# Two operands of the seven-product layer kept in PSUM, and five output pieces in another order

## The chip, the cores and the metric

The kernel runs on one core of a Trainium2 chip. The time is device microseconds (us) of one execution; the median of several runs counts. All arithmetic that readers will meet is float32, much of it as pairs of a rounded high part and a low part.

## What is computed

The reference chains a retention (linear attention) layer, a dense mixture of four experts and a gated feed-forward layer:

```
x = attention(q, k, v, lam)                      # 1536 x 512
for e in range(4):                               # p: the normalized gate of a token
    h = max(x @ w1[e], 0)                        # 512 -> 1024
    out += p[:, e:e+1] * (h @ w2[e])             # 1024 -> 512
h = out @ w_in                                   # 512 -> 2048
return (h * sigmoid(h)) @ w_out                  # 2048 -> 512
```

## The kernel before, in words

The 1536 tokens are three blocks of 512. One block goes through the experts as plain products (phase "a", `gemm1` and `gemm2`), the other two go through them together (phase "c"); for the last layer these are phases "b" and "d". Each product is three matmuls of float32r parts: high by high, low by high, high by low.

In phases c and d the first layer of a pair of weight blocks is a Strassen form: seven products instead of eight, 1, 5, 6, 7, 3, 2, 4 in that order, each of six matmuls of 128x512 (`product`, L749). They accumulate in four PSUM banks that the program names x, y, z and v. Phase c has 16 pairs. The first eight (`pair_step`, L823) do the second layer plainly: eight pieces a pair, one for each of two token blocks t and four column blocks d (`down`, L794); piece d uses bank po`d`, and VectorE adds the bank to the accumulator one unit later (L817). The second eight pairs of phase c and all eight of phase d (`pair7`, L1008) use seven products for the second layer too (`down7`, L961). Its seven operands are sums of the activated blocks v, z, x, y. Operand 6 is v minus a sum, operand 4 is y minus operand 6.

Each operand is split in two steps by `operand` (L935): ScalarE rounds the source into `hhi` or `ohi` (L939), and VectorE, for operand 5 GpSimd, subtracts that from the source into `hlo` or `olo` (L941). Before the change operands 6 and 4 stand in the SBUF tile s2 (`second`, L1043, and L1126), so that VectorE's subtraction for them reads SBUF twice. In the profile this tile is called s, as are the SBUF copies of z and y that `copied` makes (L1019).

The banks change roles from pair to pair: the next pair's y is this pair's v, and the next v is this y (L1014). A pair begins its y with ScalarE's copy of x into that bank (L1053); the sixth product adds onto it. Between the products `filler` (L744) pops one second-layer piece from the list `fill` and then `unit` (L736) issues what is due, as the adding of a bank. The order within an engine is the order of the code (manual schedule): every engine runs its instructions in that order, and an instruction that waits holds those behind it.

At the first pair of the second form (pair 8 of phase c) `fill` holds 12 pieces: four with t = 0 of pair 6, d = 0 to 3, and eight of pair 7, t = 1 before t = 0. Line 1326 puts the four t = 1 pieces of pair 7 behind the first one, because `second_form` may close a pool of tiles after the last of them; one piece is popped behind each product.

Of the kernel before, what the change touches and what calls it, by code (L numbers as in the profile page):

```python
# [7 lines left out]
F32 = mybir.dt.float32  # L8
# [7 lines left out]
P = 128  # L16
# [9 lines left out]
TW = 512  # L26
# [13 lines left out]
def kernel(  # L40
# [189 lines left out]
    def flush():  # L230
        while pending:
            pending.pop(0)()
# [296 lines left out]
    tmp = {}  # L529
# [199 lines left out]
    fill = []  # L729
# [3 lines left out]
    def after(n, fn):  # L733
        due.append((clock[0] + n, fn))
# [9 lines left out]
    def filler():  # L744
        if fill:
            fill.pop(0)()
        unit()
# [187 lines left out]
    def operand(i, r, src, eng=nc.vector):  # L935

        kind = "h" if free["h"] and (r in (1, 5, 6) or not free["o"]) else "o"
        hi, lo, done = take(kind)
        nc.scalar.activation(out=hi, in_=src, func=AF.Copy)  # L939
        op_t[i, r] = hi, lo, done  # L940
        return lambda: eng.tensor_tensor(  # L941
            out=lo, in0=src, in1=hi.bitcast(F32), op=ALU.subtract
        )

    def vadd(out, a, b, op=ALU.add, eng=nc.vector):
        eng.tensor_tensor(out=out, in0=a, in1=b, op=op)  # L946
# [61 lines left out]
    def pair7(i, prepare, plan_n=None):  # L1008

        ph = now["ph"]  # L1010
        key = (ph, now["first"] + i)
        order = roles[0]
        x, y, z, v = (psum.tile([P, TW], F32, tag=f"ps{order[r]}", name=r) for r in "xyzv")
        roles[0] = {"x": order["z"], "y": order["v"], "z": order["x"], "v": order["y"]}  # L1014
        s, low, sig = {}, {}, {}

        def copied(name, src):
            s[name] = tmp["s"].tile([P, TW], F32, tag=f"s{name}", name=f"s{name}")
            nc.scalar.activation(out=s[name], in_=src, func=AF.Copy)  # L1019

        def gated(name, c):
            if ph == "d":
                sig[name] = tmp["d"].tile([P, TW], F32, tag="sg", name="sg", bufs=3)
                nc.scalar.activation(out=sig[name], in_=c, func=AF.Sigmoid)

        def times(name, c):
            to = c
            if name == "z":
                if ph == "c":
                    sig["z"] = tmp["d"].tile([P, TW], F32, tag="sg", name="sg")  # L1030
                to = sig["z"]
            if ph == "d":
                vadd(to, c, sig[name], ALU.mult)
            else:
                nc.vector.scalar_tensor_tensor(
                    out=to, in0=c, scalar=0.0, in1=gate_t["c", key[1] // 4, int(name in "vz")],
                    op0=ALU.max, op1=ALU.mult,
                )

        def high(r, c, eng=nc.vector):  # L1040
            low[r] = operand(i, r, c, eng)

        def second(a, b):  # L1043
            s[2] = tmp["d"].tile([P, TW], F32, tag="s2", name="s2")
            minus(s[2], a, b)

        def minus(to, a, b):
            vadd(to, a, b, ALU.subtract)

        plan = [  # L1050
            (
                (1, x, True),
                [lambda: nc.scalar.activation(out=y, in_=x, func=AF.Copy)],  # L1053
                0,
                [],
            ),
            ((5, z, True), [lambda: copied(5, z)], 1, []),
            ((6, y, False), [lambda: copied(16, y)], 1, []),
            (
                (7, y, False),  # L1060
                [lambda: vadd(v, y, s[5]), lambda: gated("v", v)],
                1,
                [lambda: times("v", v), lambda: high(3, v)],
            ),
            (
                (3, z, False),
                [lambda: vadd(z, z, s[16]), lambda: gated("z", z), lambda: low[3]()],
                1,
                [
                    lambda: times("z", z),  # L1070
                    lambda: minus(z, v, sig["z"]),
                ],
            ),
            (
                (2, x, False),
                [
                    lambda: gated("x", x),
                    lambda: high(7, z),
                    lambda: times("x", x),
                    lambda: high(1, x),  # L1080
                    lambda: low[7](),
                ],
                1,
                [
                    lambda: low[1](),
                    lambda: minus(sig["z"], sig["z"], x),
                    lambda: second(v, sig["z"]),
                ],
            ),
            (  # L1090
                (4, y, False),
                [
                    lambda: gated("y", y),
                    lambda: high(5, sig["z"], nc.gpsimd),
                    lambda: high(6, s[2]),
                    lambda: low[5](),
                ],
                2,
                [
                    lambda: times("y", y),  # L1100
                    lambda: high(2, y),
                    lambda: low[6](),
                    lambda: low[2](),
                ],
            ),
        ]
        for gap, ((r, to, begin), then, n, later) in enumerate(plan):
            if gap == 6 and i % 2:
                fill.extend(
                    (lambda m=m, d=d: down7(i // 2, m, d)) for m in range(7) for d in range(2)  # L1110
                )
            if plan_n:
                n = plan_n[gap]
            product(key, r, to, begin)
            for fn in then:
                fn()
            for job in prepare.get(gap, ()):
                job()
            for k in range(max(n, 1)):
                if n:  # L1120
                    filler()
                if k == 0:
                    for fn in later:
                        fn()

        minus(s[2], y, s[2])  # L1126
        after(2, lambda: high(4, s[2]))
        after(3, lambda: low[4]())

    def jobs_for(key, following):  # L1130

        jobs = {}
        if key[1] < SW:
            jobs[5 if key[1] < SW - 1 else 3] = [lambda: split_down(key)]
        if key[1]:
            jobs[0] = [lambda: left_second(key)]
        if following:
            jobs[2] = [lambda: left_sums(following)]
            jobs[4] = [lambda: left_first(following)]
        return jobs  # L1140
# [12 lines left out]
    with tc.manual_schedule():  # L1153
# [75 lines left out]
        for i in range(NN, na):  # L1229
            gi, f = steps["a"][i]  # L1230
# [72 lines left out]
        for i in range(NW):  # L1303
            jc = jobs_for(("c", i), ("c", i + 1) if i + 1 < NW else None)
            if i % 4 == 3:
                for gap, t in ((5, 1), (6, 0)):
                    jc.setdefault(gap, []).append(lambda t=t: load_gate("c", i // 4 + 1, t))
            if i < SW:
                for gap, fn in ((0, flush), (1, 0), (3, flush), (4, 0)):
                    if not fn:  # L1310
                        if (i, gap) == (0, 1) or i == SW - 1:
                            continue
                        fn = lambda: decode_next(True)
                    jc.setdefault(gap, []).append(fn)
                if i == SW - 2:
                    jc.setdefault(6, []).extend([flush, lambda: decode_next(True)])
                elif i == SW - 1:
                    jc[4].append(store_decoded)
                pair_step("c", i, jc)
                continue  # L1320
            if i == SW:
                flush()
                store_decoded()
                words.close()
                tmp["op"] = pool(ops, "opsp")
                fill[:] = fill[:1] + fill[4:8] + fill[1:4] + fill[8:]
                last_old = fill[4]
                fill[4] = lambda: (last_old(), second_form())
                jc[5] = jc.get(5, []) + [lambda: down_sums(0)]
                jc[6] = jc.get(6, []) + [lambda: down_sums(1)]  # L1330
            elif i == SW + 1:
                for gap, qs in ((0, [0]), (1, [1]), (3, [2]), (4, [3]), (6, [4, 5])):
                    jc.setdefault(gap, []).extend(lambda q=q: down_left(q) for q in qs)
            if i == NW - 1:
                jc[4] = [lambda: split_up(("b", 0), False)]
            pair7(i - SW, jc, {SW: [1] * 7, SW + 1: [0, 1, 1, 1, 1, 1, 2]}.get(i))

        for _ in range(3):
# [151 lines left out]
```

## Time and profile before

| what | us |
|---|---|
| median of 3 runs | 795.23 |
| the three runs | 788.44, 795.26, 795.23 |
| the profiled execution | 795.96 |
| its span, first to last instruction | 794.1 |
| TensorE busy in the span | 780.4 (98%) |
| VectorE busy | 571.3 (72%) |
| ScalarE busy | 363.4 (46%) |
| GpSimd busy | 504.8 (64%) |

The profiled execution has 1.86 us outside its span, and it is 0.73 us longer than the median. TensorE is named PE in the rows, VectorE DVE, ScalarE ACT, GpSimd POOL. Times in the rows are us from the span's start. A start and a length in a row of the timeline belong to one instruction or to several alike that follow each other; what stands in brackets is the idle time of the engine before it and what ended that.

### The profile page before, as it was taken

The page shows a single profiled execution, that of the slowest core. Times are in us where ns is not written, and L with a number is a line of the kernel's source. Part 1 is how long each engine was busy: PE and PEld are TensorE (multiplying, and loading weights), DVE is VectorE, ACT ScalarE, POOL GpSimd, SP SyncE. Part 2 cuts the span into 40 slices and gives each one's busy share as a digit, 9 for nine tenths or more (in the row PEclk, how much of TensorE's full clock was granted, in tenths as well). Part 3 has the DMA queues.
Part 4 walks back from the last instruction along what each step waited for, and adds up shares of the span by engine and source line. Part 5 has one row for each costly group of instructions (what it writes and reads, how often), then busy time and mean ns, then how long its engine had stood idle before and what let it go on. Part 6 is the DMA issues. An engine that isn't in the chain of part 4 may idle for free.

```text
span 794.1 us, 11059 instructions
## 1 busy us (share of the span) xinstructions
PE 780.4 (98%) x4038; PEld 646.4 (81%) x4038; DVE 571.3 (72%) x812; ACT 363.4 (46%) x648; POOL 504.8 (64%) x458
## 2 busy tenths in 40 slices
PE   8999999999999999998997999999999999999998
PEld 8888888888888888887886888888888787888886
DVE  7345587786586788888687887875455478888885
ACT  3323434334455344434352545454454476565651
POOL 3856655353775455555695898977777855666643
PEclk9999999999999999999999999999999999999999
DMA  8868668543244344333002120203867525232302
GB/s 296 317 226 249 223 214 294 197 170 101 93 146 133 132 151 142 132 104 108 29 27 79 40 95 26 80 27 136 294 237 286 181 92 173 66 128 81 123 1 107
DMA packets 39912, 113.89 MB, mean 143 GB/s; under 512 B 4482, under 2 KB 6706, under 8 KB 39858
## 3 DMA queue, kind: packets, MB, share of 16 engines
q1 hardware_dynamic: 39856, 113.18, 41.7%
q8 instruction: 32, 0.52, 0.3%
q14 instruction: 22, 0.18, 0.1%
q10 hardware_dynamic: 2, 0.00, 0.0%
HBM read 89.02 MB, written 24.14 MB: 143 GB/s over the span
## 4 chain that ended last, share of the span: by engine, by line
PE 80%; DVE 14%; ACT 3%; POOL 2%; issue 1%; ACTq 0%; POOLq 0%
PE po L981 19%; PE ph L553 17%; PE po L609 17%; PE y L755 9%; PE z L755 5%; PE x L755 5%; DVE acc L817 3%; PE po L803 3%; ACT hhi L782 2%; PE s L419 2%; PE xps L458 2%; DVE hlo L785 2%; DVE dec L213 1%; DVE dec L217 1%; DVE hlo L941 1%
## 5 line engine op out<-in xcount | busy, mean ns | idle before, releaser
L150 POOL TENSOR_TENSOR ub<-u,ua 128x1024 fp32r<-128x1024 f32 (+2 forms) x41 | 70.2, 1712 | 111.6 <-ACT ua L149 106.2
L150 POOL TENSOR_TENSOR dl<-d,dh 128x1024 fp32r<-128x1024 f32 (+1 forms) x33 | 78.5, 2381 | 24.6 <-ACT dh L149 24.5
L150 POOL TENSOR_TENSOR ub<-us,ua 128x1024 fp32r<-128x1024 f32 x23 | 56.0, 2435 | 28.7 <-ACT ua L149 28.7
L579 ACT ACTIVATE hhi<-ph 128x512 fp32r<-128x512 f32 x40 | 23.9, 599 | 104.1 <-DVE ph L573 85.1
L609 PE MATMUL po<-hhi,dh 128*128 128x512 f32 (+1 forms) x208 | 57.2, 379 | 0.0
L609 PE MATMUL po<-hhi,dl 128*128 128x512 f32 (+1 forms) x208 | 55.9, 373 | 0.0
L609 PE MATMUL po<-hlo,dh 128*128 128x512 f32 (+1 forms) x208 | 55.8, 372 | 0.0
L553 PE MATMUL ph<-xhi,ua 128*128 128x512 f32 (+1 forms) x208 | 53.3, 378 | 1.2 <-ACT ua L149 1.2
L803 PE MATMUL po<-hhi,dh 128*128 128x512 f32 x128 | 50.4, 394 | 2.6 <-DVE acc L817 2.6
L553 PE MATMUL ph<-xhi,ub 128*128 128x512 f32 (+1 forms) x208 | 52.3, 373 | 0.0
L553 PE MATMUL ph<-xlo,ua 128*128 128x512 f32 (+1 forms) x208 | 52.1, 372 | 0.0
L803 PE MATMUL po<-hhi,dl 128*128 128x512 f32 x128 | 50.3, 393 | 0.0
L803 PE MATMUL po<-hlo,dh 128*128 128x512 f32 x128 | 50.3, 393 | 0.0
L946 DVE TENSOR_TENSOR acc<-po,acc 128x512 f32<-128x512 f32 x56 | 37.9, 684 | 13.6 <-PE po L981 13.6
L580 DVE TENSOR_TENSOR hlo<-ph,hhi 128x512 fp32r<-128x512 f32 x40 | 27.7, 692 | 27.4 <-ACT hhi L579 27.4
L817 DVE TENSOR_TENSOR acc<-po,acc 128x512 f32<-128x512 f32 x56 | 37.0, 682 | 14.3 <-PE po L803 14.3
L553 PEld LDWEIGHTS ph<-xhi,ua 128*128 128x128 f32 x208 | 36.8, 188 | 8.9 <-ACT xhi L474 1.4
L946 DVE TENSOR_TENSOR a<-po,a 128x512 f32<-128x512 f32 (+1 forms) x50 | 33.6, 675 | 14.5 <-PE po L981 14.1
L149 ACT ACTIVATE dh<-d 128x1024 fp32r<-128x1024 f32 (+2 forms) x52 | 40.1, 792 | 7.6 <-PE po L609 3.1
L609 PEld LDWEIGHTS po<-hhi,dl 128*128 128x128 f32 x208 | 37.8, 188 | 7.0
L609 PEld LDWEIGHTS po<-hlo,dh 128*128 128x128 f32 x208 | 37.8, 188 | 7.0
L609 PEld LDWEIGHTS po<-hhi,dh 128*128 128x128 f32 x208 | 37.1, 188 | 7.5 <-issue 0.2
(218 smaller groups left out, 2182.0 us busy)
## 6 DMA issues: line engine op xcount, KB each, us to landing
u<-wts SPq DMA_DIRECT2D x32, 512.0 KB, 3.5
d<-wts SPq DMA_DIRECT2D x32, 512.0 KB, 4.2
words<-wts SPq DMA_DIRECT2D x32, 512.0 KB, 4.8
wd<-dec SPq DMA_DIRECT2D x32, 256.0 KB, 2.7
d<-wd SPq DMA_DIRECT2D x16, 512.0 KB, 3.6
qkt<-qk SPq DMA_DIRECT2D x12, 512.0 KB, 4.3
kvt<-kv SPq DMA_DIRECT2D x10, 512.0 KB, 4.8
u<-wd SPq DMA_DIRECT2D x8, 512.0 KB, 4.0
```

The source lines that it names most:

```text
L149: nc.scalar.activation(out=hi, in_=src, func=AF.Copy)
L150: eng.tensor_tensor(out=lo, in0=src, in1=hi.bitcast(F32), op=ALU.subtract)
L419: nc.tensor.matmul(s[t, p // n][:, p % n], lhsT=qkt[r, 1, p], rhs=qkt[r, 0, p], start=True, stop=True,)
L553: nc.tensor.matmul(pt[:, :n], lhsT=w, rhs=x[:, k, o:o + n], start=(j == 0), stop=(j == len(ops) - 1),)
L579: nc.scalar.activation(out=hi, in_=pt, func=AF.Copy)
L580: nc.vector.tensor_tensor(out=lo, in0=pt, in1=hi.bitcast(F32), op=ALU.subtract)
L609: nc.tensor.matmul(po_t[d][:, o:o + n], lhsT=w[:, d * P:(d + 1) * P], rhs=h[:, :n], start=(begin and j == 0), stop=(last and j == 2), skip ...
L755: nc.tensor.matmul(to, lhsT=a[:, k * P:(k + 1) * P], rhs=b[:, k], start=(first and j == 0), stop=(j == len(ops) - 1), skip_group_check=not ...
L803: nc.tensor.matmul(po, lhsT=w, rhs=h, start=(j == 0), stop=(j == len(ops) - 1))
L817: nc.vector.tensor_tensor(out=a, in0=po, in1=a, op=ALU.add)
L946: eng.tensor_tensor(out=out, in0=a, in1=b, op=op)
L981: nc.tensor.matmul(po[:, part], lhsT=w, rhs=h[:, part], start=(fresh and j == 0), stop=(j == len(ops) - 1), skip_group_check=not fresh,)
```

## The change

Operand 6 is now written over the block v in its PSUM bank, and operand 4 over the block y in its bank. Operand 4 still needs operand 6, so ScalarE copies the sum from v into the SBUF tile s2 (`copied`, with the pool as a new argument). The list `fill` at pair 8 is put in another order: of pair 7's t = 1 pieces d = 1 and d = 2 come before d = 0; d = 3 stays the last of them.

```diff
-        def copied(name, src):
-            s[name] = tmp["s"].tile([P, TW], F32, tag=f"s{name}", name=f"s{name}")
+        def copied(name, src, to="s"):
+            s[name] = tmp[to].tile([P, TW], F32, tag=f"s{name}", name=f"s{name}")
             nc.scalar.activation(out=s[name], in_=src, func=AF.Copy)
...
-        def second(a, b):
-            s[2] = tmp["d"].tile([P, TW], F32, tag="s2", name="s2")
-            minus(s[2], a, b)
...
                     lambda: minus(sig["z"], sig["z"], x),
-                    lambda: second(v, sig["z"]),
+                    lambda: minus(v, v, sig["z"]),
...
                     lambda: high(5, sig["z"], nc.gpsimd),
-                    lambda: high(6, s[2]),
+                    lambda: high(6, v),
+                    lambda: copied(2, v, "d"),
                     lambda: low[5](),
...
-        minus(s[2], y, s[2])
-        after(2, lambda: high(4, s[2]))
+        minus(y, y, s[2])
+        after(2, lambda: high(4, y))
         after(3, lambda: low[4]())
...
-                fill[:] = fill[:1] + fill[4:8] + fill[1:4] + fill[8:]
+                fill[:] = fill[:1] + fill[5:7] + fill[4:5] + fill[7:8] + fill[1:4] + fill[8:]
```

On ScalarE, from the end of pair 9 of phase c to the start of pair 10, there stood (s_4021 is the tile s2 of pair 9, the L149 rows split weights, and `y<-x` begins the next pair):

```order
L939 ACTIVATE hhi<-s_4021 128x512
L149 ACTIVATE dh<-d_3511 128x256
L149 ACTIVATE dh<-d_3638 128x256
L149 ACTIVATE dl<-d_3511 128x256
L149 ACTIVATE dl<-d_3638 128x256
L939 ACTIVATE hhi<-y 128x512
L149 ACTIVATE dw<-d_3511 128x256
L149 ACTIVATE dw<-d_3638 128x256
L1053 ACTIVATE y<-x 128x512
L149 ACTIVATE uc<-u_3717 128x512
L939 ACTIVATE ohi<-s_4021 128x512
```

At the same place there stands now (s_4035 is s2):

```order
L939 ACTIVATE hhi<-v 128x512
L1019 ACTIVATE s_4035<-v 128x512
L149 ACTIVATE dh<-d_3511 128x256
L149 ACTIVATE dh<-d_3638 128x256
L149 ACTIVATE dl<-d_3511 128x256
L149 ACTIVATE dl<-d_3638 128x256
L939 ACTIVATE hhi<-y 128x512
L149 ACTIVATE dw<-d_3511 128x256
L149 ACTIVATE dw<-d_3638 128x256
L1049 ACTIVATE y<-x 128x512
L149 ACTIVATE uc<-u_3717 128x512
L939 ACTIVATE ohi<-y 128x512
```

One instruction is new in the row, the copy of v into s2, ahead of the weight splits and of the next pair's `y<-x`; the two roundings read v and y instead of s2.

On VectorE at the end of pair 9 there stood:

```order
L941 TENSOR_TENSOR hlo<-s_4021,hhi 128x512
L941 TENSOR_TENSOR hlo<-y,hhi 128x512
L946 TENSOR_TENSOR acc<-po,acc 128x512
L946 TENSOR_TENSOR s_4021<-y,s_4021 128x512
L941 TENSOR_TENSOR olo<-s_4021,ohi 128x512
```

Now:

```order
L941 TENSOR_TENSOR hlo<-v,hhi 128x512
L941 TENSOR_TENSOR hlo<-y,hhi 128x512
L946 TENSOR_TENSOR acc<-po,acc 128x512
L946 TENSOR_TENSOR y<-y,s_4035 128x512
L941 TENSOR_TENSOR olo<-y,ohi 128x512
```

No instruction is added or moved on VectorE; the two subtractions that read SBUF twice now read a PSUM bank and SBUF. The rows of TensorE read alike before and after, since they show neither the column block nor the bank of a piece.

## Rows read from the trace of the kernel before

**Rows 1.** Waits of TensorE: us in total, times, longest.

```profile
PE y L755 <- ACT s L1019: 4.2, 1, 4.2
PE po L803 <- DVE acc L817: 2.6, 1, 2.6
...
PE y L755 <- ACT y L1053: 0.5, 1, 0.5
```

**Rows 2.** Windows: length, busy PE PEld DVE ACT POOL, clock, DMA, GB/s.

```profile
364.00:384.00 20.00, 17.45 (x72) 14.01 (x71) 11.44 (x18) 5.75 (x10) 10.64 (x9) 0.91 0.31 93
...
404.00:424.00 20.00, 15.81 (x70) 12.79 (x69) 19.01 (x21) 9.86 (x21) 17.98 (x22) 1.00 0.20 73
424.00:444.00 20.00, 20.00 (x82) 16.34 (x81) 14.93 (x23) 8.36 (x15) 12.76 (x13) 0.91 0.02 6
```

**Rows 3.** Timeline of TensorE in pair 8: start, length, line, operation.

```profile
373.84 0.61 PE L755 MATMUL z<-lo,ua 128*128 128x512 f32 x2
377.01 0.77 PE L803 MATMUL po<-hhi,dh 128*128 128x512 f32 x1 [2.56 <-DVE acc L817]
...
379.70 0.80 PE L755 MATMUL y<-hi,ua 128*128 128x512 f32 x2
```

**Rows 4.** Timeline of VectorE, pairs 7 and 8.

```profile
364.39 1.88 DVE L817 TENSOR_TENSOR acc<-po,acc 128x512 f32<-128x512 f32 x3
...
375.57 0.69 DVE L785 TENSOR_TENSOR hlo<-y,hhi 128x512 fp32r<-128x512 f32 x1 [0.66 <-ACT hhi L782]
376.18 0.68 DVE L817 TENSOR_TENSOR acc<-po,acc 128x512 f32<-128x512 f32 x1
```

**Rows 5.** Timeline of ScalarE in pair 8.

```profile
375.43 0.59 ACT L1053 ACTIVATE y<-x 128x512 f32<-128x512 f32 x1
```

**Rows 6.** Timeline of TensorE in pair 10.

```profile
417.97 0.61 PE L981 MATMUL po<-ohi,dw 128*128 128x512 f32 x2
...
419.10 0.39 PE L981 MATMUL po<-hlo,dw 128*128 128x512 f32 x1
423.68 0.73 PE L755 MATMUL y<-hi,ua 128*128 128x512 f32 x2 [4.19 <-ACT s L1019]
...
428.12 0.63 PE L755 MATMUL z<-hi,ua 128*128 128x512 f32 x2
```

**Rows 7.** Timeline of VectorE, end of pair 9.

```profile
411.16 0.69 DVE L946 TENSOR_TENSOR s<-v,sg 128x512 f32<-128x512 f32 x1
...
412.96 7.23 DVE L941 TENSOR_TENSOR hlo<-s,hhi 128x512 fp32r<-128x512 f32 x1
...
421.32 0.68 DVE L946 TENSOR_TENSOR s<-y,s 128x512 f32<-128x512 f32 x1
```

**Rows 8.** Timeline of ScalarE in pair 10.

```profile
423.04 0.59 ACT L1019 ACTIVATE s<-y 128x512 f32<-128x512 f32 x1
```

**Rows 9.** Timeline of GpSimd, pairs 9 and 10.

```profile
412.26 1.29 POOL L941 TENSOR_TENSOR hlo<-sg,hhi 128x512 fp32r<-128x512 f32 x1
...
419.72 1.06 POOL L690 TENSOR_TENSOR us<-us,u 128x256 f32<-128x256 f32 x1
```

**Rows 10.** Line 941: count, ns least/median/most, first and last start.

```profile
L941 DVE TENSOR_TENSOR olo<-s,ohi x24: 693/932/1703, 395.3 to 776.8; 128x512 fp32r<-128x512 f32 x24
...
L941 DVE TENSOR_TENSOR olo<-y,ohi x15: 677/689/692, 396.0 to 773.8; 128x512 fp32r<-128x512 f32 x15
...
L941 DVE TENSOR_TENSOR hlo<-s,hhi x8: 691/790/7229, 413.0 to 738.5; 128x512 fp32r<-128x512 f32 x8
```

**Rows 11.** ScalarE's start of y, first handover and the tightest.

```profile
395.88 0.59 ACT L1053 ACTIVATE y<-x 128x512 f32<-128x512 f32 x1
...
644.07 0.58 ACT L1053 ACTIVATE y<-x 128x512 f32<-128x512 f32 x1
```

**Rows 12.** TensorE's sixth product into that y.

```profile
397.57 0.61 PE L755 MATMUL y<-hi,ua 128*128 128x512 f32 x2
...
645.23 0.62 PE L755 MATMUL y<-hi,ua 128*128 128x512 f32 x2
```

## The prediction

> **What bounds the kernel now.** I read the waits of TensorE first, then windows of 20 us along the span, then the timelines of all engines around the two windows that stand out. The waits show an engine that hardly ever stops: in the stretch that the change touches, two waits of 4.2 and 2.6 us are the large ones, and each occurs once [rows 1]. The windows add what follows a stop. From 364 to 384 us and from 424 to 444 us the granted clock is 0.91, where the window between them that holds the longer stop has 1.00 [rows 2]: part of the stretch behind each stop ran at the lower of the two levels, 1.2 GHz, and only the rest at 2.4 GHz. So the kernel ends when TensorE's queue ends, and a change is worth what it takes from TensorE's stops and from the slow matmuls behind them. VectorE, ScalarE and GpSimd have idle time to give.
>
> A full-speed matmul of 128x512 takes 0.226 us of the queue: from 417.97 to 419.10 five were started [rows 6]. A product or a piece of six is therefore 1.36 us.
>
> **Stop one, and the new order of pieces.** In pair 8 the last two matmuls of a product start at 373.84, so the next piece was due at 374.29. It started at 377.01, released by VectorE's adding of a bank [rows 3]. The reason is the bank: the piece in front, pair 6's d = 0, and this one, pair 7's d = 0, both use po0. The adding that frees po0 stands in VectorE's queue behind the subtraction at 375.57 and ran from 376.18 [rows 4]. In the new order the piece behind the first is d = 1. Its bank po1 was emptied in the three addings at 364.39 [rows 4], and its operands are those of the same pair and half as before; so it starts at 374.29 and ends its turn at 375.65. po0 now comes third, after two products and a piece more.
>
> What is late next is the product into y. It needs ScalarE's copy of x into y, which ran from 375.43 and took 0.59 us, to 376.02 [rows 5]; nothing in the new order makes that earlier. With 0.03 us for the signal the product starts at 376.05 instead of 379.70 [rows 3]: a gain of 3.65 us, with a stop of 0.4 us left. The nearest row for such a rest is the wait of 0.5 us for the same kind of copy [rows 1]. From both sides: if the copy comes 0.6 us later, 3.05; if it were hidden, 4.05 and another 0.2 or so, as the late product started at a slow clock. I take 3.65, which goes by the rows of this very place.
>
> **Stop two, and the operand in PSUM.** At the end of pair 9 VectorE's subtraction for operand 6, both inputs in SBUF, took 7.23 us from 412.96 [rows 7]. The same instruction takes 0.69 us at its least, and those that read y in PSUM never took over 0.692 us in 15 times; the 24 and 8 with the operand in SBUF have medians of 0.932 and 0.790 and reach 1.703 and 7.229 [rows 10]. GpSimd had work without a gap beside it: nine of its instructions follow each other from 412.26 to 419.72, and the tenth, which was the one under way when VectorE got through, took 1.06 us [rows 9]. Behind the held subtraction VectorE's queue waited, so operand 4 was formed only at 421.32 [rows 7]; ScalarE, which had to round operand 4 next, could copy y for product 7 only at 423.04 [rows 8]; and TensorE, due at 419.33, started product 7 at 423.68 [rows 6]. That is 4.35 us. The twelve matmuls from there took until 428.12 [rows 6], 4.44 instead of 2.72 us: another 1.72 us at the slow clock. Together 6.07 us.
>
> With v in PSUM the subtraction has one SBUF input, like the rows that never stretched. I take 0.69 us for it. VectorE is then free about 6.5 us sooner and operand 4 is formed near 416; the copy of y then waits for TensorE's sixth product alone, and is ready before product 7 is due. The gain is 6.07 us. Its ends are zero, if the hold has another cause, and the whole 6.07. The other 31 subtractions also get shorter by the medians, 24 x 0.24 and 7 x 0.1 us, but no wait of TensorE hangs on them, and I count them at nothing.
>
> The Trainium skill, page "SBUF — State Buffer", section "Who interferes with whom", says that a VectorE instruction with two SBUF inputs contends with a GpSimd instruction that reads SBUF, and that whoever issues first has the shared ports for that whole instruction. The trace agrees with the first half and not with the second: by the rule the wait ends with the one GpSimd instruction that was running, at 413.55 [rows 9], and would be 0.6 us, while the row says some 6.5 us [rows 7]. By the rule the rest of the hold is from something that the change may leave alone; this is the first rival below.
>
> **What the change adds.** Sixteen copies on ScalarE, one a pair, 0.59 us each by the row of such a copy [rows 8]. In the changed program VectorE's subtraction from v waits for this copy too, since both read the bank v, and the next pair's copy of x into that bank waits for the subtraction. Behind it on ScalarE stand weight splits, the rounding of operand 4 and the two copies that products 6 and 7 need. So what has to hold is the handover from pair to pair, fourteen of them. At the first, y was ready at 396.47 [rows 11] and used at 397.57 [rows 12], 1.10 us of slack; at the tightest, in phase d, it was 644.65 against 645.23, 0.58 us. The other twelve lie at or above the first, as I read them from pairs of rows like these. The chain gets one copy longer, 0.5 to 0.6 us, and the subtraction in it shorter by 0.0 to 0.9. Only the tightest handover can stop TensorE, for at most 0.1 us. From both sides: nothing, or, if each handover came 1.2 us later, 0.1 us at the first and 0.6 at the tightest. I take 0.
>
> Writing over v and y in PSUM in place of s2 adds nothing in count. The bank y is held until operand 4 is split, three units into the next pair; the next writing of it is behind product 7 there, four products on. These edits cost nothing as long as that order holds.
>
> **The sum.** 3.65 + 6.07 = 9.72 us from the profiled execution's 795.96 gives 786.24. That execution was 0.73 us over the median of the runs shown, so I predict 785.5 us, 1.2% less. The fastest of the three runs, 788.44, is 6.8 us under the others. That is close to what stop two costs, and I take it to be an execution without the long hold. From it the sum would be 788.44 - 3.65 = 784.8, near the same.
>
> **The rivals.** *The hold stays.* If VectorE was held by something other than its two SBUF inputs, for instance on the side of its output, then operand 6 in PSUM is held as before, and only the order of pieces pays: 795.23 - 3.65 = 791.6. For it: one event, and the long hold is not what a single GpSimd instruction explains. Against it: subtractions with a PSUM input stay at 0.69 us in all their rows [rows 10]. Chance 0.12.
>
> *The order only moves the stop.* The d = 1 piece goes ahead, but the product into y is as late as before, or po0 stops the third piece. Then 795.23 - 6.07 = 789.2. For it: the copy into y is indeed late by 0.4. Against it: it doesn't depend on the piece. Chance 0.08.
>
> *The handover becomes the bound.* If the chain rounding, copy, subtraction, copy of x (0.6 + 0.6 + 0.7) lies wholly behind what it was, and one more large ScalarE instruction of about a microsecond gets in between, y is 2.9 us late at each of fourteen handovers. With the first handover's slack of 1.10 for all, that costs 14 x 1.8 = 25 us, less the 9.7 gained: 810 us. It decides from a lateness of 1.1 + 9.7/14 = 1.8 us on, below which the change is still not slower. For it: ScalarE runs strictly in order and now waits for VectorE at each pair's end. Against it: my working finds a lateness of 0.6. Chance 0.06.
>
> **Chances and range.** Forecast 0.70, hold 0.12, moved stop 0.08, handover 0.06; 0.04 for the rest, a smaller stop of 2 to 4 us somewhere new. A measurement can tell about 1% from no change, here 787.3 us. The forecast's own range, 783.8 to 787.2, is below it; the two partial cases are above it. So faster 0.72, the same 0.22, slower 0.06. For 8 in 10 the low end is 783.8, with the small rests of stop one and of the tightest handover gone too; the high end is 790.0, which takes in the moved stop and leaves out the hold and the handover, 0.18.
>
> **What would show it.** In the changed kernel's profile the wait of 4.2 us for ScalarE's copy and that of 2.6 us for the adding should be gone, with a wait of about 0.4 us for the copy into y in pair 8; no window should show a clock of 0.91 there. All subtractions of line 941 on VectorE should be 0.68 to 0.70 us. It would be wrong if one of them is held, if TensorE waits for the copy into y in several pairs, or if the gaps go and the span doesn't follow.

## The result and the profile after

The changed kernel takes 786.12 us in the median of 13 runs (784.89 to 787.42). The kernel before, run in turn with it, takes 795.23 us (787.79 to 803.83, 13 runs). The medians differ by 9.1 us, and 785.5 was predicted where 786.1 was measured. The ratio, taken over the fast runs and so without the one at 803.83, is 0.990 with an interval of 0.988 to 0.993: faster by 1.0%, some 7.9 us.

The spread is part of the result. All runs of the changed kernel lie within 2.5 us of each other, those of before within 16. Over all the comparisons below the kernel before ran 97 times: 51 runs lie under 792 us, with a median of 789.6, 39 from 792 to 799, and 7 above that. I call runs of the first kind undisturbed; what makes the others longer is called the event below.

The profiled execution has a span of 784.5 us, 9.6 less than before. TensorE's waits in it (us in total, times, longest):

```profile
PE y L755 <- ACT y L1049: 0.7, 2, 0.4
PE po L981 <- ACT acc L628: 0.6, 1, 0.6
```

The waits of 4.2 and 2.6 us of [rows 1] are gone; the wait for the copy of x into y now occurs twice, at the start of phase d, where it stood before too, and in pair 8. In the windows (span, busy time of TensorE, granted clock, share of the DMA engines, GB/s) no clock of 0.91 is left where [rows 2] had two:

```profile
364.00:384.00 20.00, 19.71 (x87) 1.00 0.34 93
404.00:424.00 20.00, 20.00 (x90) 1.00 0.22 79
424.00:444.00 20.00, 20.00 (x90) 1.00 0.11 39
```

The place of stop one, TensorE's timeline in pair 8 (start, length, instruction, idle time before it and its releaser):

```profile
373.74 0.62 PE L755 MATMUL z<-lo,ua 128*128 128x512 f32 x2
374.20 0.39 PE L803 MATMUL po<-hhi,dh 128*128 128x512 f32 x1
...
375.33 0.39 PE L803 MATMUL po<-hlo,dh 128*128 128x512 f32 x1
376.01 0.73 PE L755 MATMUL y<-hi,ua 128*128 128x512 f32 x2 [0.29 <-ACT y L1049]
...
377.50 0.39 PE L803 MATMUL po<-hhi,dh 128*128 128x512 f32 x1
```

The piece starts when it is due, 0.46 us behind the last two matmuls of the product, where [rows 3] shows it held up. The product into y comes at 376.01 instead of 379.70, and waits a little for the copy. The piece behind that product starts at 377.50; in the kernel before it was this row:

```profile
381.25 0.39 PE L803 MATMUL po<-hhi,dh 128*128 128x512 f32 x1
```

The place of stop two, VectorE at the end of pair 9, which answers to [rows 7]:

```profile
409.30 0.69 DVE L941 TENSOR_TENSOR hlo<-v,hhi 128x512 fp32r<-128x512 f32 x1
411.01 0.69 DVE L941 TENSOR_TENSOR hlo<-y,hhi 128x512 fp32r<-128x512 f32 x1 [1.02 <-ACT hhi L939]
...
412.21 0.69 DVE L946 TENSOR_TENSOR y<-y,s 128x512 f32<-128x512 f32 x1
```

The subtraction for operand 6 took 0.69 us instead of 7.23, and the difference y, operand 4, was formed at 412.21 instead of 421.32. The durations of line 941 on VectorE (ns: least, median, longest) hold for the whole span:

```profile
L941 DVE TENSOR_TENSOR olo<-v,ohi x27: 680/692/693, 383.8 to 763.3; 128x512 fp32r<-128x512 f32 x27
L941 DVE TENSOR_TENSOR olo<-y,ohi x27: 679/692/694, 392.3 to 767.1; 128x512 fp32r<-128x512 f32 x27
...
L941 DVE TENSOR_TENSOR hlo<-v,hhi x5: 681/692/692, 409.3 to 504.5; 128x512 fp32r<-128x512 f32 x5
```

No subtraction takes over 0.694 us. The place by itself doesn't show that the operand's bank is the cause, since GpSimd's row of work is another one here too. Behind the subtraction for operand 5 it now has a gap, in which it waits for ScalarE's split of weights; that split now stands behind the new copy:

```profile
408.10 1.29 POOL L941 TENSOR_TENSOR hlo<-sg,hhi 128x512 fp32r<-128x512 f32 x1 [0.44 <-ACT hhi L939]
409.65 1.44 POOL L150 TENSOR_TENSOR dh<-d,dh 128x256 fp32r<-128x256 f32 x2 [0.27 <-ACT dh L149]
```

The experiments below set the operand's place apart from that gap. On TensorE product 7 of this pair starts at 415.58, 8.10 us earlier than in [rows 6], and the product after it at 418.30, 9.82 earlier:

```profile
414.22 0.62 PE L981 MATMUL po<-ohi,dw 128*128 128x512 f32 x2
...
415.58 0.62 PE L755 MATMUL y<-hi,ua 128*128 128x512 f32 x2
...
418.30 0.62 PE L755 MATMUL z<-hi,ua 128*128 128x512 f32 x2
```

Of the 9.82 us, 0.10 were there ahead of stop one (373.84 against 373.74). Behind it the lead was 3.75 us (381.25 against 377.50), and it was still 3.75 just ahead of stop two (417.97 against 414.22). So stop one gave 3.65 us and stop two 6.07.

### The profile page after: what moved, and what is told of

It reads as the page before. It is cut to its first block, busy times and chain, and to the rows that moved or that the text cites. A ratio compares the mean times of both kernels' runs of the same rounds, so it can differ in the third digit from the quotient of the medians.

```text
span 784.5 us, 11076 instructions
## 1 busy us (share of the span) xinstructions
PE 777.6 (99%) x4038; PEld 644.4 (82%) x4038; DVE 558.4 (71%) x812; ACT 370.3 (47%) x664; POOL 496.8 (63%) x458
## 4 chain that ended last, share of the span: by engine, by line
PE 83%; DVE 12%; ACT 3%; issue 2%; ACTq 0%; DVEq 0%
PE po L981 19%; PE po L609 17%; PE ph L553 16%; PE y L755 10%; PE x L755 6%; PE z L755 6%; PE po L803 4%; DVE acc L817 3%; PE s L419 2%; ACT hhi L782 2%; PE xps L458 2%; DVE hlo L785 1%; DVE dec L213 1%; DVE dec L217 1%; DVE dec L207 1%
## 5 line engine op out<-in xcount | busy, mean ns | idle before, releaser
L149 ACT ACTIVATE dh<-d 128x1024 fp32r<-128x1024 f32 (+2 forms) x52 | 40.2, 796 | 7.8 <-issue 2.9
```

## The experiments

My theory was that of the prediction: the order is worth 3.65 us, the operand in PSUM 6.07 because VectorE reading SBUF twice is held while GpSimd works, and the copies on ScalarE cost nothing. The rivals were those of the prediction, and on the hold itself several.

**The order alone** (the kernel before with only the new line of `fill`):

```diff
-                fill[:] = fill[:1] + fill[4:8] + fill[1:4] + fill[8:]
+                fill[:] = fill[:1] + fill[5:7] + fill[4:5] + fill[7:8] + fill[1:4] + fill[8:]
```

> The kernel before with the new order of the five pieces alone; the operands stay in SBUF. My theory (two separate gains): the wait of 2.6 us for the bank's adding is gone in pair 8 and a wait of 0.3 to 0.4 us for the copy into y is left, worth some 3.6 us. The hold of a subtraction with two SBUF inputs can still strike, as in the kernel before, so the runs spread over several us as before's do; a median of 791.6 us, between 786 and 800 in single runs. The rival (the order only moves the stop): a wait of over 2 us stays in pair 8, and the time is that of before, 795.

Measured: a median of 786.5 us (10 runs), ratio to before 0.995 (0.990 to 1.000), before at 789.8 in these comparisons. I had expected a median of 791.6, and the one measured misleads: six runs lie from 785.4 to 786.7, as those of the changed kernel do, and four at 789.6, 790.5, 793.1 and 796.8. The profile fell on a run without a long hold, and its subtractions from SBUF still stretch:

```profile
L941 DVE TENSOR_TENSOR olo<-s,ohi x24: 693/987/1704, 391.4 to 766.8; 128x512 fp32r<-128x512 f32 x24
```

So the order pays: its undisturbed runs lie at 786.2 us, those of the kernel before at 789.6. The four longer runs, by 3 to 11 us, are where I take a long hold to have struck; none of them was profiled.

**PSUM alone** (the changed kernel with the old line of `fill`, the diff above reversed).

> The changed kernel with the old order of the five pieces; the operands are in PSUM. My theory: the wait of 2.6 us for the bank's adding in pair 8 is back with a granted clock of about 0.91 in its 20 us, no subtraction of line 941 on VectorE is over 0.70 us, and the runs lie close together: 786.1 + 3.6 = 789.7 us, all within 788.5 to 791. The rival (the hold has another cause and only its moment has moved): a hold of several us returns in some runs, which then spread over 788 to 800.

Measured: 789.94 us (788.59 to 790.18, 10 runs), ratio to before 0.998 (0.995 to 1.001). The stop in pair 8 is back, with its slow clock (a wait, then the window from 364 to 384 us):

```profile
PE po L803 <- DVE acc L817: 2.6, 1, 2.6
```

```profile
364.00:384.00 20.00, 17.42 (x71) 0.91 0.32 93
```

To the changed kernel it is 789.94 - 786.12 = 3.8 us: the price of the order, undisturbed. And 789.9 is where the kernel before lies in its undisturbed runs (789.6). The operand in PSUM doesn't make the undisturbed run faster; it keeps it undisturbed.

**The operand from its SBUF copy** (everything as changed, but VectorE reads s2 instead of v for operand 6):

```diff
-            out=lo, in0=src, in1=hi.bitcast(F32), op=ALU.subtract
+            out=lo, in0=kept() if kept else src, in1=hi.bitcast(F32), op=ALU.subtract
...
-                    lambda: high(6, v),
+                    lambda: high(6, v, nc.vector, lambda: s[2]),
```

> The changed kernel, but VectorE's subtraction for operand 6 reads ScalarE's SBUF copy of the sum in place of the bank v; ScalarE, the order and everything else stay as changed. My theory (two SBUF inputs beside GpSimd): of these 16 subtractions several are over 0.75 us again and one may be held for several us where GpSimd's queue has no gap; operand 4's sixteen stay at 0.69. The times spread upwards: a median between 786 and 795, with single runs over 790. The rival (the hold comes from the output side or from GpSimd alone): all 16 stay at 0.69 and the time is 786.1, as close together as the changed kernel's.

Measured: a median of 786.28 us, but four of the ten runs are at 791.1, 791.5, 792.4 and 792.5; the other six lie from 785.1 to 786.6. One source of 16 subtractions, moved back from PSUM to SBUF, brings the longer runs back, by about 6 us each. Its profile fell on the fastest run and had no long hold. What a meeting with GpSimd costs there is seen in pair 13, on VectorE and then on GpSimd:

```profile
484.54 1.64 DVE L941 TENSOR_TENSOR olo<-s,ohi 128x512 fp32r<-128x512 f32 x1
```

```profile
484.34 1.29 POOL L941 TENSOR_TENSOR hlo<-sg,hhi 128x512 fp32r<-128x512 f32 x1
485.59 3.28 POOL L150 TENSOR_TENSOR dw<-d,dw 128x256 fp32r<-128x256 f32 x4
```

VectorE came 0.2 us behind GpSimd's instruction, waited until that one ended, and went through: 1.64 us.

**The hold by itself.** A small kernel, with VectorE's sum of two SBUF tiles issued behind the start of 4, 8 or 16 GpSimd sums.

> The hold by itself; the whole of the reference's computation is left out. A chain of GpSimd sums of 128x256 runs back to back; behind the first GpSimd result VectorE has one sum of 128x512 to make. With two SBUF inputs and chains of 4, 8 and 16 sums (0.7 us each): my theory is that VectorE gets through only at the end of the chain, so its sum takes about 3.5, 6.5 and 12 us; with an idle place before the seventh sum of 16 (GpSimd waits for ScalarE there) it takes about 5 us; with one input in PSUM 0.69 us whatever the chain; with a single SBUF input not over 0.7 us. The rival (one GpSimd instruction has the ports, then the other engine gets them): at most about 1.5 us in every one of the chains.

Measured (durations on VectorE; the third row is the sum with no chain beside it, the last has one input in PSUM):

```profile
L63 DVE TENSOR_TENSOR held_four<-first_four,base 128x512 f32<-128x512 f32 x1 | 1.2, 1195 | 1.4 <-POOL first_four L63 1.4
...
L63 DVE TENSOR_TENSOR held_sixteen<-first_sixteen,base 128x512 f32<-128x512 f32 x1 | 1.2, 1195 | 1.4 <-POOL first_sixteen L63 1.4
...
L63 DVE TENSOR_TENSOR held_alone<-first_alone,base 128x512 f32<-128x512 f32 x1 | 0.7, 692 | 1.4 <-POOL first_alone L63 1.4
...
L63 DVE TENSOR_TENSOR held_psum<-bank,first_psum 128x512 f32<-128x512 f32 x1 | 0.7, 691 | 1.4 <-POOL first_psum L63 1.4
```

My theory that the hold lasts to the end of the chain falls: whatever the chain, it lasted one instruction. With one input in PSUM there is none. A tensor_scalar with a single SBUF input took 0.929 us where I had expected at most 0.7; that miss I did not follow up.

**The moment of the meeting.** The same with the sizes and types of pair 9, the moment of issue shifted in steps, first 44 meetings, later 240.

> The hold by itself once more, in 44 rounds, with the shapes and types of the long hold in the kernel before: GpSimd subtractions of 512, six of 256, 512 and four of 256 elements back to back, and one VectorE subtraction of 512 with two SBUF inputs that is issued 0.02 us later from round to round; in the last four rounds its first input is in PSUM. The whole of the reference's computation is left out. The last micro kernel showed a hold of one GpSimd instruction, always asked for at the same moment. Theory A (the moment decides): at most moments the subtraction gets in behind the GpSimd instruction under way (0.7 to 2.0 us), at a few it misses several and takes 3 us or more. Theory B (one instruction always, so the long hold needs something else that runs in the kernel): none over 2.0 us. In PSUM 0.69 us.

> A kernel of its own; what the reference asks for is left out. 240 times VectorE's subtraction with two SBUF inputs beside GpSimd's burst of the sizes and types of pair 9 (1.3, six of 0.7, 1.3, four of 0.7 us), its moment of issue moved in steps of a few ns over about one microsecond and a half. Theory C, the long hold is a rare outcome of that meeting alone, a race for the port: a few of the 240 take 3 us or more, the rest 0.7 to 2. Theory D, the meeting alone always costs one GpSimd instruction and the long hold needs something that only the whole kernel has: all 240 between 0.68 and 2.0 us.

Measured in the first and in the second (ns: least, median, longest; the row with bank has one input in PSUM):

```profile
L66 DVE TENSOR_TENSOR held<-zeros,hi x40: 680/1238/1643, 5.7 to 513.0; 128x512 fp32r<-128x512 f32 x40
L66 DVE TENSOR_TENSOR held<-bank,hi x4: 679/681/682, 524.9 to 562.5; 128x512 fp32r<-128x512 f32 x4
```

```profile
L66 DVE TENSOR_TENSOR held<-zeros,hi x240: 681/1208/1641, 5.7 to 3108.6; 128x512 fp32r<-128x512 f32 x120
```

In 280 meetings VectorE never lost more than the rest of one GpSimd instruction. None of the moments tried makes a long hold by itself. So something that only the whole kernel has seems to come in, which isn't shown.

**More copies on ScalarE** (two, then four more of v into s2 at each pair's end, for the rival of the handover):

```diff
                     lambda: copied(2, v, "d"),
+                    lambda: nc.scalar.activation(out=s[2], in_=v, func=AF.Copy),
+                    lambda: nc.scalar.activation(out=s[2], in_=v, func=AF.Copy),
```

> The changed kernel with ScalarE's copy of operand 6 made three times over instead of once at each pair's end (two copies more, 0.5 us each in the queue). My theory of the slack at the handovers: 1.0 us later, four handovers with 0.8 to 0.9 us of slack stop TensorE for 0.1 to 0.2 us, the tightest for 0.9, the others not: 1.6 us in all, 787.8 us. The rival (the added copy sits on the path of every pair): 16 us more, 802.

> The same with four copies more, 2.0 us later. By the slacks: four handovers stop TensorE for 1.1 to 1.2 us, the tightest for 1.9, one for 0.8, the eight with 1.9 us of slack and an idle ScalarE before them not or hardly: 7.4 us, 793.5 us. The rival (every pair): 32 us more, 818.

Measured: 790.77 us with two (8 runs), 808.02 with four (2 runs, ratio to before 1.021, 1.013 to 1.029). TensorE's waits in the first and in the second:

```profile
PE y L755 <- ACT y L1049: 3.1, 7, 1.2
```

```profile
PE y L755 <- ACT y L1049: 12.2, 16, 2.5
```

I missed both, 787.8 and 793.5 were expected, and the rival's 802 and 818 miss them from the other side. A part of the miss is my price of a copy. The one copy of the change starts 0.50 us behind the rounding ahead of it (408.68 in the changed kernel's trace), and I took that for each further one. But the added copies start 0.63 us apart, as the kernel with four shows on ScalarE:

```profile
391.51 0.60 ACT L1093 ACTIVATE s<-v 128x512 f32<-128x512 f32 x1
392.14 0.60 ACT L1094 ACTIVATE s<-v 128x512 f32<-128x512 f32 x1
```

So the handovers come 1.25 and 2.5 us later instead of 1.0 and 2.0. Their stops then follow from the slack that each had. With two copies the four handovers with 0.8 to 0.9 us of slack start TensorE's product 0.4 to 0.5 us late and the tightest 1.35; the eight with 1.94 us keep about 0.9 or 1.0. With four copies all sixteen starts are late, two of them (pair 8 and the start of phase d) as in the changed kernel. Added up and less the changed kernel's own, these delays are 3.3 us with two copies and 13.7 with four, of 4.7 and 21.9 us of time. The rest isn't traced; the profile with two copies fell on the slowest of its runs (792.79), and the one with four has a window at a clock of 0.91 (640 to 660 us). The one copy of the change stays within the slack, but for 0.10 us at the tightest handover.

**Removing the small rests** (another placing of a piece in pair 8, and of a weight job in phase d):

```diff
-            pair7(i - SW, jc, {SW: [1] * 7, SW + 1: [0, 1, 1, 1, 1, 1, 2]}.get(i))
+            pair7(i - SW, jc, {SW: [1, 2, 1, 1, 1, 1, 0], SW + 1: [0, 1, 1, 1, 1, 1, 2]}.get(i))
...
-            lefts = {0: (1,), 2: (2,), 5: (3,)} if i == 1 else {2: (0, 1), 5: (2,)}
+            lefts = {0: (1,), 2: (2,), 6: (3,)} if i == 1 else {2: (0, 1), 5: (2,)}
```

> The changed kernel with two of its rests taken out: in pair 8 two pieces instead of one before the product into y, and none at the pair's end, so that the copy into y is hidden; and in the second pair of phase d the weight split of the fourth operand one product later, so that ScalarE empties the bank that TensorE waits for 0.6 us sooner. My theory: the waits of 0.3 us in pair 8 and of 0.6 us for ScalarE's copy at line 628 go, 0.9 us less, 785.2 us. The rival (the split is late for its product, or the stop only moves on): 786 or more.

Measured: 786.26 us (785.54 to 786.45, 12 runs), no gain to the 786.12; 785.2 was expected. The wait of 0.6 us at line 628 is gone. The one in pair 8 moved to the next handover (0.20 us at 393.67), and a wait for the copy s is new:

```profile
PE y L755 <- ACT y L1049: 0.6, 2, 0.4
PE y L755 <- ACT s L1019: 0.2, 1, 0.2
```

No version here beats the changed kernel.

**GpSimd without a gap** (two subtractions for one set of down weights done twice in pair 9, once with operand 6 from the SBUF copy, once from PSUM):

```diff
             split(nc.gpsimd, t[:, s, 0], t[:, s, 1], src)
+            if twice:
+                nc.gpsimd.tensor_tensor(out=t[:, s, 1], in0=src, in1=t[:, s, 0].bitcast(F32), op=ALU.subtract)
```

> The changed kernel with operand 6 subtracted from the SBUF copy, and with GpSimd's two subtractions for one set of down weights done twice in pair 9 (1.4 us more, the same values), so that GpSimd has no idle time from its subtraction for operand 5 to the end of its nine instructions, as in the kernel before. Theory E, the hold ends only where GpSimd's queue has a gap: nearly all runs near 792, and a profile with a hold of 6 to 9 us in pair 9. Theory D as in the small kernels, one instruction: all near 786.3. Theory C, chance: a mixture as in the kernel without the doubling, 4 of 10 near 792.

> The changed kernel with the same doubling of GpSimd's two subtractions in pair 9, operand 6 in PSUM as changed. All theories: near 786.1 in all runs, no subtraction of line 941 on VectorE over 0.70 us. If it has runs near 792, the doubling itself costs them and the other kernel of this pair tells nothing.

Measured: 792.45 us from the copy, nine of ten runs from 792.2 to 794.9 and one at 785.8; 786.04 from PSUM (785.22 to 787.61, 10 runs). The two kernels differ in nothing but the operand's place. The extra GpSimd work costs nothing by itself, and with the SBUF source it makes the event the rule: 6.4 us. And this time the profile caught it, on VectorE, GpSimd and TensorE. It was not in pair 9, where the work was doubled and where theory E put it (the subtraction took 0.97 us there, from 408.79), but in pair 13; why the doubling brings it on there is open:

```profile
484.89 7.76 DVE L943 TENSOR_TENSOR olo<-s,ohi 128x512 fp32r<-128x512 f32 x1
492.57 0.68 DVE L943 TENSOR_TENSOR olo<-y,ohi 128x512 fp32r<-128x512 f32 x1
```

```profile
484.68 1.31 POOL L943 TENSOR_TENSOR hlo<-sg,hhi 128x512 fp32r<-128x512 f32 x1
485.92 2.85 POOL L150 TENSOR_TENSOR dw<-d,dw 128x256 fp32r<-128x256 f32 x4
488.71 1.46 POOL L150 TENSOR_TENSOR dh<-d,dh 128x256 fp32r<-128x256 f32 x2
490.09 1.33 POOL L150 TENSOR_TENSOR uc<-u,uc 128x512 fp32r<-128x512 f32 x1
491.33 0.76 POOL L690 TENSOR_TENSOR us<-u 128x256 f32<-128x256 f32 x1
492.17 1.06 POOL L690 TENSOR_TENSOR us<-us,u 128x256 f32<-128x256 f32 x1
```

```profile
491.00 0.39 PE L983 MATMUL po<-hlo,dl 128*128 128x512 f32 x1
496.11 1.22 PE L755 MATMUL y<-hi,ua 128*128 128x512 f32 x2 [4.72 <-ACT s L1021]
```

This is stop two of [rows 6 to 9] once more, in another pair. VectorE stood through nine GpSimd instructions and got through at `us<-us,u`, which took 1.06 us: the same instruction, with the same length, as in [rows 9]. It is the first of the burst that needs the result of the one before it, and GpSimd pauses 0.08 us ahead of it, from 491.33 + 0.76 to 492.17. And an unbroken row of GpSimd work isn't enough to begin a long hold, so that half of theory E falls: pair 13 has the same unbroken burst in the kernel without the doubling (the trace of the operand from its SBUF copy, above). VectorE came 0.20 us behind its start there and 0.21 here, and it was let through after one instruction there and after nine here.

**Breaks in GpSimd's queue** (the kernel of the doubling with the SBUF source; behind each set of down weights GpSimd adds 128x8 elements of what it has just written, some 60 times):

```diff
+        b = t[:, 1, 1][:, :8].bitcast(F32)
+        c = tmp["op"].tile([P, 8], F32, tag="brk", name="brk", bufs=1)
+        nc.gpsimd.tensor_tensor(out=c, in0=b, in1=b, op=ALU.add)
         dw_t[q] = t
```

> The kernel of the doubled subtractions with operand 6 from the SBUF copy, in which 9 of 10 runs were near 792 to 795; in addition, behind every two subtractions of a set of down weights, GpSimd adds 128x8 elements of what it has just written (a scratch tile, read by nobody), so that its queue has a real break every 1.4 to 2.8 us, at some 60 places. Theory F, a hold once begun lasts to GpSimd's first break, an instruction that needs the one before it: no run near 792, all 785.5 to 787.5, and the profile's longest subtraction of line 941's kind with the operand in SBUF is at most 4.2 us, ending at such an addition. Theory C, how long a hold lasts has nothing to do with breaks: runs near 792 as often as before, and a hold of 6 us or more in the profile if it falls on such a run. If all subtractions are under 1.7 us and no run is near 792, breaks remove the long hold, but where a hold ends is then shown only by the two long ones seen.

Measured: 789.1 us, and all 12 runs between 788.24 and 789.93, where without the additions 9 of 10 were over 6 us longer than the tenth. The longest subtraction:

```profile
L946 DVE TENSOR_TENSOR olo<-s,ohi x12: 701/903/1666, 391.6 to 766.0; 128x512 fp32r<-128x512 f32 x12
```

The event is gone, as the theory of the breaks says, but the run is not the expected 785.5 to 787.5: the 56 additions that the trace has (0.2 us each) come with about 3 us more than the undisturbed 786, spread over the pairs, and I did not trace how. They also shift every later moment, so this supports that a break ends a hold and does not prove it. By the third outcome written beforehand, where a hold ends is shown by the two long ones alone.

## Why the prediction was right, and where it was not

*Stop one, 3.65 us.* Right, and for the reason given: 3.65 at the place, 3.8 in the runs that differ in the order alone. The rest was predicted at 0.4 us; the product into y started 0.45 behind its due time (375.33 and one matmul of 0.23 against 376.01). The 0.03 us put in for the signal was 0.05 here (the copy of x into y ended at 375.96). The rival by which the order only moves the stop falls.

*Stop two, 6.07 us.* Right in size, 6.07 at the place, and in its cause, which the place alone doesn't show: the operand's place in SBUF or PSUM. With it in SBUF 17 of 30 runs were more than 3 us over the undisturbed ones (the order alone, the SBUF copy, the doubling with it), with it in PSUM none of 45 (the changed kernel, PSUM alone, the moved rests, the doubling with it). The plainest comparison is the doubling: 9 of 10 against 0 of 10. The rival by which the hold stays falls. What I had wrong is its nature. The step reads "I take it to be an execution without the long hold", of the 788.44 us; that fits the undisturbed runs, which lie from 787.2 to 791.1, but I treated this as the exception and the hold as the state of the kernel. Over the 97 runs, 51 were without it. The gain in the median depends on which runs one draws: 9.1 us here, while against the 789.8 that the kernel before had in the next comparison it would be 3.7. Mean against mean, the 90 runs of before up to 799 us at 792.15 and the 13 of after at 786.12, it is 6.0. That the gain in the median came out near 9.7 is luck of the draw. The predicted time held because the working came to nearly the same point from either kind of run, 785.5 and 784.8.

*The length of the hold.* The prediction set the trace against the Trainium skill's page "SBUF — State Buffer", section "Who interferes with whom", by which the port is held for one instruction. In 280 meetings of the small kernels, and nearly all in the full one, the rule agrees with the traces: at most 1.7 us in all. In two profiled cases it does not: 7.23 and 7.76 us, through nine GpSimd instructions each. Both ended at the first instruction of GpSimd's row that depends on the one before. What begins such a hold stays open; a like moment and burst gave 1.64 us in one run and 7.76 in another.

*The copies at nothing.* Right for the sum. The tightest handover, in phase d, on ScalarE, VectorE and TensorE:

```profile
633.26 0.59 ACT L1019 ACTIVATE s<-v 128x512 f32<-128x512 f32 x1
...
634.67 0.58 ACT L1049 ACTIVATE y<-x 128x512 f32<-128x512 f32 x1 [0.33 <-DVE olo L941]
```

```profile
633.89 0.69 DVE L941 TENSOR_TENSOR olo<-v,ohi 128x512 fp32r<-128x512 f32 x1 [0.56 <-ACT s L1019]
```

```profile
634.76 0.61 PE L755 MATMUL z<-lo,ua 128*128 128x512 f32 x2
635.31 0.73 PE L755 MATMUL y<-hi,ua 128*128 128x512 f32 x2
```

VectorE now waits 0.56 us for the copy, as foreseen. TensorE's product starts 0.10 us behind its due time of 635.21, as much as I had put it at, and too little to be counted as a wait. The second wait for the copy into y, of 0.4 us, is another one: it stands at the first pair of phase d and was 0.5 before [rows 1].

```profile
620.12 0.73 PE L755 MATMUL y<-hi,ua 128*128 128x512 f32 x2 [0.37 <-ACT y L1049]
```

I had the copy make each handover 0.5 to 0.6 us later, less what the subtraction gains. By the traces it was 0.22 at the first (0.88 us of slack left of 1.10), 0.39 to 0.44 at four more, 0.62 at the tightest, and nothing at the eight that had 1.94 before and after.

*The rival of the handover.* The change is well short of it. Its working had the first handover's slack for all fourteen, though, and that is not what the runs show: eight of them have more. The 808 us with four copies comes near the rival's 810, but from stops that add up to 13.7 us where it had 25. That two copies more measured level with before (ratio 0.999, 0.995 to 1.003) rests on the disturbed runs of before; to its undisturbed 789.6 they are 1.2 us slower.

*The sum.* 9.72 us predicted from the profiled execution. Its two parts were there in full, 9.6 were left at the end of the span, and from profiled execution to profiled execution it is 795.96 - 786.24 = 9.72. That the last agrees to the hundredth is chance.

## What to carry to other kernels

In this kernel a VectorE subtraction with both inputs in SBUF, beside a long row of GpSimd work, had a price with a tail: usually at most the rest of one GpSimd instruction, in two profiled cases nine of them. Moving one input to PSUM took the tail away. Before pricing a stall from one profile, look at the spread of the runs: a median between two kinds of runs says more on the draw than on the kernel. And a chain is to be priced by the slack of each of its handovers: one copy more was free here, but two further ones stopped TensorE at the five handovers with less than a microsecond left, and four at all of them.

## What was not expected of the hardware

- The profiles show holds of two kinds: at most 1.7 us in all, or 7.2 and 7.8 us, the shorter and the longer beside the same row of GpSimd instructions. The long one was seen only in the full kernel, in two traces; none came in 280 meetings alone.
- Beside TensorE's full load, VectorE's 128x512 subtraction in float32 took 0.68 to 0.69 us whether its source was in PSUM or, undisturbed, in SBUF; there was no price for reading PSUM.
